# Splitting five exponentials, with their sums and transposes, into two groups in the first unit, and moving a weight sum to GpSimd

## The chip, the cores and the metric

The kernel runs on one core of one Trainium2 chip. The metric is the device time of one execution in microseconds (us), taken as the median of several executions. A profile records one execution; its times count from the start of the span, which is some 2 us shorter than the device time.

Most runs of one kernel lie within 1.6 us of its median, but 11 of the 73 runs come out 5.7 to 7.6 us longer, with the kernel before and with the variants alike (one more, of 939.03, lies between). Two traces that fell on such runs show that the extra time arises in the first 50 us, ahead of everything discussed here (see the last section). I call them late starts.

## The reference, cut to what matters

Eight batches of attention with pooled keys and values, then a two-layer network with a "snake" activation:

```python
k_p, v_p = means of k, v over 8 neighbouring rows        # 576 -> 72 rows
scores = q @ k_p^T / 8; scores -= max(scores)
attn = exp(scores) / sum(exp(scores))
x = (attn @ v_p), heads side by side                      # 4608 x 512
h = x @ w_in                                              # 512 -> 2048
g = h + sin(alpha * h)**2 / alpha
out = g @ w_out                                           # 2048 -> 512
```

Both large products are done by a fast matrix-multiplication scheme (seven products of sub-blocks instead of eight), so sums of blocks of `w_in` are needed before some of the products.

## The kernel before

The first layer runs in nine units of 512 rows. A unit has 28 slots: four groups J of seven products, 8 matmuls each in the trace. Everything else is attached to a slot, and runs in the order in which it is emitted, each engine taking its own work strictly in that order. In the first unit (u = 0) attention for "batch two" (index 1) has to be done beside the products, because the second unit needs its result.

```python
def exp(i):                                   # row block i of five; ScalarE
    nc.scalar.activation(out=e, in_=e, func=AF.Exp, scale=scale)
def norm(i):                                  # sum and reciprocal on VectorE, multiplication (L280) on GpSimd
    nc.vector.tensor_reduce(out=sm[:n], in_=ex[:n, i, :, 0:Sp + 1], axis=AX, op=OP.add)   # L287
    divide(i, sm, nc.gpsimd)
def turn(i):                                  # two 32x32-block transposes on VectorE (L404, L405)
    ...
def move(part):                               # SBUF to SBUF, 8 transfers for each part, all five blocks in each (L416)
    ...
# ... one group G of a unit, the work left over after product k of the slot before:
def left0(): nc.scalar.copy(out=G.b6[:], in_=G.b1[:])                  # L692; then the squares of group Q before
def left1(): self.finish(Q)                                            # L733, two additions on VectorE
def left2(): nc.scalar.copy(b7 <- b6); nc.scalar.copy(p5 <- b5)        # L704, L706
def left3(): sin(G, 0, 0, G.b1); square(G, 0, 0)                       # ScalarE L672, L679
def left4(): add(G.g[:, 1, :, 1], G.b7[:], G.p5[:])                    # L645: must be read before product 4 writes b7
# ... the schedule of the first unit:
at(8, self.combine_w_in, 2, (0, 1, 2, 3), self.nc.gpsimd)              # third part of w_in, four additions (L537)
at(13, self.combine_w_in, 3, (0, 1, 2, 3))                             # fourth part, on VectorE
for i in range(5):
    at((4, 5, 6, 7, 8)[i], A.q_t, i)
    at((7, 8, 9, 11, 12)[i], A.score, i)
    at((14, 14, 15, 15, 15)[i], A.exp, i)
    at((14, 15, 15, 16, 16)[i], A.norm, i)
    at((15, 16, 16, 17, 17)[i], A.turn, i)
# ...
at(17, A.move, 0); at(17, A.move, 1)
at(20, A0.norm_rest); at(23, A0.a_rest)                                # remainder of batch one (L359 to L368, L394)
at(25, lambda: A.values((0, 2, 1, 3), A.free_banks()))                 # products with the values (L456, L458)
```

`Sin` and `Exp` lie in different activation tables. A switch shows in the trace as ACT_TABLE_LOAD; `Square` and copies run between exponentials without one.

## Time and profile before

| | before |
|---|---|
| median | 937.49 us (936.88 to 937.92, 3 runs) |
| profiled span | 935.2 us, clock 0.995 |
| TensorE busy | 914.5 us, 98% |
| waits of TensorE between 64 and 81 us | 1.20 + 0.35 + 5.12 us |
| matmuls at half clock after them | 6.50 us for what takes 3.46 elsewhere |

A "wait" is idle time of an engine just before an instruction; behind the arrow stands what ended it by the profile. With TensorE busy nearly throughout, only its waits (and its clock) can be won. The prediction shows the lines.

### The profile page before, as it was taken

To read this page: it belongs to the slowest core of one execution; us is meant where nothing else is said; L and a number is where in the kernel's file an instruction comes from. 1 tells how busy PE (TensorE), PEld (TensorE's weight loads), DVE (VectorE), ACT (ScalarE), POOL (GpSimd) and SP (SyncE) were. 2 spreads that over 40 slices of the span, in tenths; PEclk is the share of its full clock that TensorE was granted. 3 is DMA by queue.
4 is the path that set the end of the run, shared out by engine and by line. 5 is a ranking of instruction groups with operands and counts; after the bars stand their busy time and mean duration, and the time that the engine had idled before them with its cause. 6 is when DMAs were issued, how large, how long until landed. Compare 5 with 4: busy or idle time off the path is not lost.

```text
span 935.2 us, 17656 instructions
## 1 busy us (share of the span) xinstructions
PE 914.5 (98%) x6953; PEld 817.3 (87%) x6953; DVE 690.6 (74%) x1064; ACT 436.9 (47%) x1009; POOL 152.6 (16%) x150
## 2 busy tenths in 40 slices
PE   7997999999999999999999999999999999999997
PEld 6675787887878788787888899999999999999997
DVE  7578675766757677573456889988888898889794
ACT  3664576675866758677796641111121111111111
POOL 4254160341704316040000000000000000000000
PEclk9998999999999999999999999999999999999999
DMA  9964656756657565545626346252535354443501
GB/s 252 237 200 129 177 167 174 211 158 192 187 170 222 152 181 138 165 145 154 241 75 200 133 141 190 65 173 82 166 89 157 98 144 111 128 126 101 153 14 39
DMA packets 141299, 141.12 MB, mean 151 GB/s; under 512 B 49808, under 2 KB 111008, under 8 KB 141216
## 3 DMA queue, kind: packets, MB, share of 16 engines
q1 hardware_dynamic: 140144, 138.81, 51.3%
q10 hardware_dynamic: 1072, 1.19, 0.4%
q8 instruction: 55, 0.90, 0.4%
q14 instruction: 28, 0.23, 0.1%
HBM read 75.37 MB, written 47.19 MB: 131 GB/s over the span
## 4 chain that ended last, share of the span: by engine, by line
PE 93%; DVE 1%; ACT 1%; POOL 0%; issue 0%; DMA 0%; SPq 0%; DVEq 0%; ACTq 0%; POOLq 0%
PE PS L666 46%; PE PS L963 41%; PE PS L258 3%; PE PS L456 1%; PE PS L458 1%; PE PS L481 0%; ACT s L672 0%; PE PS L478 0%; POOL ex L280 0%; DVE h L733 0%; PE PS L228 0%; DVE sm L287 0%; PE PS L239 0%; DMA out_dram<-o 0%; DVE o L981 0%
## 5 line engine op out<-in xcount | busy, mean ns | idle before, releaser
L666 PE MATMUL PS<-home,a 128*128 128x256 f32 x1152 | 270.4, 386 | 5.5 <-DVE h L645 5.1
L666 PEld LDWEIGHTS PS<-home,a 128*128 128x128 f32 x1152 | 217.2, 192 | 44.1 <-DVE h L645 7.2
L666 PE MATMUL PS<-home,as 128*128 128x256 f32 x864 | 201.1, 382 | 1.2 <-ACT PS L692 1.2
L666 PEld LDWEIGHTS PS<-home,as 128*128 128x128 f32 x864 | 161.6, 190 | 25.3 <-issue 1.6
L963 PE MATMUL PS<-s,wb 128*128 128x144 f32 x896 | 119.3, 286 | 0.4 <-ACT PS L1076 0.4
L963 PEld LDWEIGHTS PS<-s,wb 128*128 128x128 f32 x896 | 113.7, 190 | 0.7 <-ACT PS L1076 0.6
L679 ACT ACTIVATE s<-s,c 128x256 f32<-128x256 f32 (+1 forms) x216 | 110.0, 572 | 0.0
L117 POOL TENSOR_TENSOR kvin<-kvin 96x768 f32<-96x768 f32 (+3 forms) x42 | 69.1, 1644 | 204.8 <-DMA kvin<-in_v_dram 191.3
L645 DVE TENSOR_TENSOR h<-PS,p 128x512 f32<-128x512 f32 x72 | 49.2, 684 | 66.4 <-PE PS L666 33.3
L672 ACT ACTIVATE s<-h,al 128x256 f32<-128x256 f32 x144 | 65.1, 502 | 56.5 <-DVE h L645 56.5
L1076 ACT COPY PS<-PS 128x144 f32<-128x144 f32 x56 | 14.7, 263 | 145.7 <-PE PS L963 144.3
L672 ACT ACTIVATE s<-PS,al 128x256 f32<-128x256 f32 x144 | 60.1, 468 | 40.1 <-DVE h L733 20.0
L963 PE MATMUL PS<-s,a 128*128 128x144 f32 x512 | 73.2, 286 | 0.0
L963 PE MATMUL PS<-r,wb 128*128 128x144 f32 x512 | 73.2, 286 | 0.0
L963 PEld LDWEIGHTS PS<-r,wb 128*128 128x128 f32 x512 | 67.1, 190 | 0.1
L963 PEld LDWEIGHTS PS<-s,a 128*128 128x128 f32 x512 | 67.0, 190 | 0.0
L733 DVE TENSOR_TENSOR h<-PS,s 128x512 f32<-128x512 f32 x36 | 24.6, 683 | 53.3 <-ACT s L679 53.2
L1095 ACT COPY PS<-PS 128x144 f32<-128x144 f32 x56 | 14.7, 263 | 88.5 <-PE PS L963 88.5
L963 PE MATMUL PS<-s,we 128*128 128x144 f32 x384 | 54.9, 286 | 0.0
L963 PE MATMUL PS<-x,wb 128*128 128x144 f32 x384 | 54.9, 286 | 0.0
L963 PEld LDWEIGHTS PS<-s,we 128*128 128x128 f32 x384 | 50.3, 190 | 0.1
L733 DVE TENSOR_TENSOR h<-h,s 128x1024 f32<-128x1024 f32 x36 | 50.3, 1398 | 0.0
(170 smaller groups left out, 1202.3 us busy)
## 6 DMA issues: line engine op xcount, KB each, us to landing
g_bridge<-h SPq DMA_DIRECT2D x72, 512.0 KB
r<-g_bridge SPq DMA_DIRECT2D x31, 1152.0 KB
out_dram<-o SPq DMA_DIRECT2D x128, 72.0 KB
kvin<-in_k_dram SPq DMA_DIRECT2D x14, 576.0 KB
q<-in_q_dram SPq DMA_DIRECT2D x7, 1024.0 KB
kvin<-in_v_dram SPq DMA_DIRECT2D x14, 512.0 KB
aM<-tr SPq DMA_DIRECT2D x56, 100.0 KB
aM<-tr SPq DMA_DIRECT2D x56, 80.0 KB
```

The costliest lines, as they stand in the source:

```text
L117: self.nc.gpsimd.tensor_tensor(out=t[..., 0:w] if w > D else out, in0=t[..., 0:w], in1=t[..., w:2 * w], op=OP.add)
L258: nc.tensor.matmul(ps[e][r:r + q.shape[-1], hp, :], q[s], k, start=True, stop=True)
L456: nc.tensor.matmul(o[64 * e:64 * e + 64], w, x, start=True, stop=False, skip_group_check=True)
L458: nc.tensor.matmul(o, w.rearrange("p e d -> p (e d)"), x, start=False, stop=True, skip_group_check=True)
L645: add = lambda o, x, y: nc.vector.tensor_tensor(out=o, in0=x, in1=y, op=OP.add)
L666: nc.tensor.matmul(ps[:, jj, :], self.A[p][:, kk, f * P:(f + 1) * P], x[:, kk, :], start=(start and jj == 0 and kk == 0), stop=(kk == 1), ...
L672: nc.scalar.activation(out=G.s[:, i, jj, j, :], in_=src[:, jj], func=AF.Sin, scale=self.al[:, f:f + 1])
L679: nc.scalar.activation(out=x, in_=x, func=AF.Square, scale=self.c[:, f:f + 1])
L733: add = lambda o, x, y: self.nc.vector.tensor_tensor(out=o, in0=x, in1=y, op=OP.add)
L963: nc.tensor.matmul(out, W[:, J // 2, J % 2, :], A[:, J, :], start=(start and J == 0), stop=(J == self.NJ - 1), skip_group_check=True)
L1076: nc.scalar.copy(out=x1[:, 0, :], in_=x0[:, 1, :])
L1095: nc.scalar.copy(out=x1[:, 1, :], in_=x1[:, 0, :])
```

## The change

The intent was to break up the burst of softmax work around slots 14 to 17. Two of the five row blocks go through exponential, sum, multiplication and transpose in slots 9 to 13, at the price of one more switch to the exponential's table and back. The fourth part of `w_in` is summed on GpSimd, so that VectorE is free for the transposes. The additions of the third part, on GpSimd already, go behind the first two multiplications (slot 10 instead of 8).

```diff
-            at(8, self.combine_w_in, 2, (0, 1, 2, 3), self.nc.gpsimd)
-            at(13, self.combine_w_in, 3, (0, 1, 2, 3))
             for i in range(5):
                 at((4, 5, 6, 7, 8)[i], A.q_t, i)
                 at((7, 8, 9, 11, 12)[i], A.score, i)
-                at((14, 14, 15, 15, 15)[i], A.exp, i)
-                at((14, 15, 15, 16, 16)[i], A.norm, i)
-                at((15, 16, 16, 17, 17)[i], A.turn, i)
+                at((9, 9, 14, 14, 15)[i], A.exp, i)
+                at((10, 10, 15, 15, 16)[i], A.norm, i)
+                at((13, 13, 16, 17, 17)[i], A.turn, i)
+            at(10, self.combine_w_in, 2, (0, 1, 2, 3), self.nc.gpsimd)
+            at(10, self.combine_w_in, 3, (0, 1, 2, 3), self.nc.gpsimd)
```

## The prediction

> **What bounds the kernel now.** I read the page first: the busy shares and the strip of 40 slices (23.4 us each).
>
> ```profile
> PE 914.5 (98%) x6953; PEld 817.3 (87%) x6953; DVE 690.6 (74%) x1064; ACT 436.9 (47%) x1009; POOL 152.6 (16%) x150
> ...
> PE   7997999999999999999999999999999999999997
> PEclk9998999999999999999999999999999999999999
> ```
>
> TensorE is the bound nearly everywhere. A change that leaves its work alone can only win where it waits. Apart from the two ends, that is the fourth slice (70 to 94 us), which is also the only one with a clock of 8 tenths. It lies in the first unit, the unit that is changed. So the second view is TensorE's timeline there (start, duration, then in brackets the idle time before it and what ended it):
>
> ```profile
> 64.20 1.89 PE L666 MATMUL PS<-home,as 128*128 128x256 f32 x8
> 67.29 1.97 PE L666 MATMUL PS<-home,as 128*128 128x256 f32 x8 [1.20 <-ACT PS L692]
> 69.09 1.89 PE L666 MATMUL PS<-home,a 128*128 128x256 f32 x8
> 71.33 1.97 PE L666 MATMUL PS<-home,a 128*128 128x256 f32 x8 [0.35 <-ACT PS L704]
> 73.13 1.89 PE L666 MATMUL PS<-home,as 128*128 128x256 f32 x8
> 80.14 6.67 PE L666 MATMUL PS<-home,a 128*128 128x256 f32 x16 [5.12 <-DVE h L645]
> 86.64 1.89 PE L666 MATMUL PS<-home,as 128*128 128x256 f32 x8
> ```
>
> Eight matmuls are one slot of the schedule; counting along the rows, 64.20 is slot 15 and 80.14 begins slot 20. Three waits: 1.20 + 0.35 + 5.12 = 6.67 us. A fourth loss is hidden in a duration: the 16 matmuls from 80.14 reach the next row after 6.50 us, where 16 such matmuls elsewhere take 3.46 (60.74 to 64.20). That is 3.04 us more. The view by windows shows why; the numbers after the window's length are busy times of PE, PEld, DVE, ACT, POOL, then the granted clock:
>
> ```profile
> 78.00:80.00 2.00, 0.00 (x0) 0.00 (x0) 1.81 (x5) 0.00 (x0) 2.00 (x2) 0.83 0.00 0
> ...
> 82.00:84.00 2.00, 2.00 (x6) 1.63 (x5) 1.97 (x2) 0.04 (x1) 1.92 (x3) 0.50 0.69 160
> ```
>
> The clock had gone to half during the wait. All there is to win here is 6.67 + 3.04 = 9.7 us, 1.0% of 937.5.
>
> What made the long wait is in the chain of waits (start, duration, engine and line):
>
> ```profile
> 66.12 0.77 DVE sm L287
> ...
> 67.26 1.16 POOL ex L280
> ...
> 71.09 2.63 DVE h L733 x2
> ...
> 77.44 1.15 POOL ex L280
> ...
> 79.51 0.59 DVE h L645
> ```
>
> Slot 20 writes into a bank which the VectorE addition L645 must have read first. VectorE takes its work in order, and ahead of that addition stand the whole of the softmax's end for batch two: five sums with reciprocals, five transposes, each of which waits for GpSimd's multiplication L280, and the additions L733. All of it starts only after the exponentials at 65.40.
>
> **What the Trainium skill says.** "TensorE: Matmul & The Clock Gate", section "What's actually happening": the array falls to half clock after an idle window of about 3.4 us and needs about 3.4 us of work to recover; the window runs freely. The trace agrees: full clock for some 4.3 us of the gap (0.83 over 78 to 80 means half clock from about 79.3), then 0.50 until about 86.1; the wait of 1.20 us cost no clock. "ScalarE: Activation LUTs", section "What ACT_TABLE_LOAD costs": about 1283 ns for the load plus 1380 ns to drain. The trace has 1.28 us, and 1.30 from the load's start to the exponential's (64.11 to 65.40); the drain is not seen as extra time here, so I use 1.28. "GPSIMD Engine Reference", section "4.1 Engine selection": two-input elementwise work is about twice as slow there as on VectorE. The trace: 1.27 us against 0.68 for the same 128x512 addition (L537). "SBUF — State Buffer", section "SBUF: two separate sides": a VectorE instruction with two SBUF inputs and a GpSimd one lock each other out for a whole instruction. The trace fits: the second L733 takes 1.21 us at 108.85, with GpSimd idle, and 2.14 at 71.56 beside L280.
>
> **The change, part by part.**
>
> *First exponentials and their table switch (new, slots 9 to 11).* ScalarE ends its work at 51.37 and then sits idle until this copy, which TensorE releases:
>
> ```profile
> 54.12 0.57 ACT L704 COPY PS<-PS 128x512 f32<-128x512 f32 x1 [2.75 <-PE PS L666]
> ```
>
> One load (1.28) and two exponentials (1.26) are 2.54 us, ending near 53.95: they fit in the 2.75. Going back to sine costs a second load. In the built program the wait for TensorE's slot 10 sits on that load, so it runs from about 55.75 to 57.05 and the sine comes 1.2 us later than its 55.84. ScalarE then waited 1.70 us for VectorE before the next sine at 59.17, so this is absorbed. Nothing reaches TensorE.
>
> *First two sums (now slot 10).* Two times (0.76 + 0.20) less overlap, about 1.75 us on VectorE from 54.95, into an idle stretch of 1.58 us before 56.53. Delay: 0.2 us, passed on down to the copy L692, so the 1.20 wait of slot 16 becomes about 1.35. The second switch to the exponentials stays in that path.
>
> *First two multiplications and both sums of w_in on GpSimd.* GpSimd is free at 56.0. Two L280 of 1.15 end at 58.3; the four additions of part three (1.27 each) end at 63.4. TensorE wants the first results in slot 15 (64.20), ready at 59.6: no wait. The four of part four end at 68.5; they are wanted only from slot 22 on.
>
> *Off VectorE.* Four L537 (2.6 us, at 62.15) disappear; in their place come two transposes of 0.92 us each (0.71 + 0.27 less overlap), which no longer wait.
>
> *What remains after 66 us.* Squares end near 68.6 as before. VectorE: two sums 66.3 to 68.1; L733 68.6 to 70.8 (0.6 + 1.2 + some 0.4 of lock; GpSimd multiplies rows two and three then, ending at 70.7 to 72.0); third transpose to 71.75; fifth sum to 72.7; GpSimd's last multiplication 72.75 to 73.95 beside the fourth transpose; fifth transpose to 75.0, or 75.4 with a full lock; L645 to 75.6 to 76.1. Before, it ended at 80.10.
>
> *TensorE.* Slot 16 at 67.45, then 1.80 per slot; the copy L704 is ready by 70.2, so the 0.35 goes. Slot 19 ends at 74.75. Slot 20 at 75.95, a wait of 1.2 instead of 5.12. That is far from 3.4 us: the clock should stay full and the 3.04 us go too.
>
> *What then comes closer.* Two things were hidden under the slow stretch. First, the remainder of batch one (L359 to L368, 3.65 us of it locked against GpSimd's pooling) is needed at slot 23. TensorE comes there at 81.2, the remainder ends about 81.6: a wait of 0.4. Second, the moves of the transposed rows:
>
> ```profile
> 79.54 10.29 SPq L416 DMA_DIRECT2D aM<-tr  x16
> ```
>
> They start when the fifth transpose ends (79.51) and the DMA strip falls quiet at about 91.1, which is 11.6 us later. From 75.2 that is 86.8. TensorE arrives at the value products (93.54 before): 82.1 + 1.8 + 0.8 + 1.9 = 86.6. A wait of about 0.3. They take 2.95 us, so slot 25's own product starts at 89.9, against 96.49 before: 6.6 us earlier by this sum. After that the work is TensorE's own as before, with the same small waits.
>
> In losses: before 9.7; after 1.35 + 1.2 + 0.4 + 0.3 = 3.25. The two ways give 6.5. I take off 0.3 for small waits that I can't see, and say 6.2.
>
> **Rivals.**
>
> *GpSimd becomes the bound of the chain.* It now has ten instructions in a row from 56.0 to 68.5 before the third multiplication, and the third transpose waits for that. For it: 1.27 us is a figure taken beside VectorE work with a PSUM input, which does not lock. Against it: VectorE has hardly any two-input SBUF work between 56 and 68.5. Two microseconds of delay would be hidden behind L733; if it came 4 us late, the wait would grow to some 3 us, the clock might drop, and the time would be about 935.
>
> *The moves take over.* For it: they need 11.6 us however early TensorE arrives; in the second unit a VectorE transpose (L194) waited 4.69 us for them. If they landed 2 us later than I think, the gain would be some 4.5 us: about 933.
>
> *The early table switch delays TensorE.* Two loads more, 2.6 us. For it: the first group ends 0.15 us before the copy L704 is due. Against: the product that needs the copy starts at 56.34. I expect nothing; at worst 1 us.
>
> *All waits close.* If the moves land early and VectorE is quicker than I have it, only the 1.35 is left: about 929.
>
> **Range and chances.** From 929.3 (nearly everything gone but the slot 16 wait) to 935.0 (the GpSimd rival, or a clock drop that stays). All that can be won is 1.0%, so over 2% faster is all but excluded; 2% slower would take 19 us of new waits in a unit of some 75 us, for which I see no source.
>
> **What would show it.** Right: in TensorE's timeline a wait of 1 to 1.5 us before slot 16, one of 0.5 to 2 us before slot 20 still released by L645, the 16 matmuls after it in about 3.5 us, clock 1.00 throughout; the eight L537 on GpSimd ending at 68 to 69; L416 issued from about 75; short waits for the remainder and the moves. Wrong: a wait of 3 us or more anywhere there with the clock at 0.50 after it, a wait for GpSimd's L537 in slots 15 to 19, or a gain that is lost again before 100 us.

## The result

The changed kernel took 930.98 us (930.28 to 931.20, 4 runs) against 937.18 for the kernel before in the same measurement (935.58 to 937.92, 4 runs): 6.2 us less. The ratio is 0.9935, with a 95% interval from 0.9918 to 0.9952. Ratios are computed as the mean time of one kernel's fast runs over that of the other's of the same rounds, so they are not quite the ratio of the medians. The interval lies clear of 1.

The page of the changed kernel, same rows as before:

```profile
PE 912.3 (98%) x6953; PEld 815.0 (88%) x6953; DVE 687.6 (74%) x1060; ACT 439.8 (47%) x1011; POOL 158.9 (17%) x154
...
PEclk9999999999999999999999999999999999999999
```

TensorE's busy time fell by 2.2 us with the same number of matmuls, and the 8 in the fourth slice of the clock is gone. That part of the gain is not a wait: it is matmuls that no longer run at half speed. (They had lost 3.04 us; a new wait of 1.1 us, shown below, counts as busy.) TensorE's timeline in the stretch (start, duration, idle time before in brackets):

```profile
64.35 1.89 PE L666 MATMUL PS<-home,as 128*128 128x256 f32 x8
67.45 1.96 PE L666 MATMUL PS<-home,as 128*128 128x256 f32 x8 [1.21 <-POOL a L537]
69.25 3.62 PE L666 MATMUL PS<-home,a 128*128 128x256 f32 x16
72.71 1.89 PE L666 MATMUL PS<-home,as 128*128 128x256 f32 x8
75.32 3.72 PE L666 MATMUL PS<-home,a 128*128 128x256 f32 x16 [0.72 <-DVE h L645]
78.87 1.89 PE L666 MATMUL PS<-home,as 128*128 128x256 f32 x8
...
85.87 3.05 PE L456 MATMUL PS<-aM,vm 64*64 64x512 f32 x16
```

The wait of 5.12 us is 0.72, the 16 matmuls behind it reach the next row after 3.55 us (78.87), and the 0.35 us before slot 18 is gone. The wait of 1.21 us before slot 16 has not moved. The last line hides a new wait: 16 value matmuls take 3.05 us where the kernel before has 1.95 (at 93.54). The chain of waits splits them:

```profile
68.60 2.19 DVE h L733 x2
...
74.68 0.59 DVE h L645
...
85.94 1.01 PE PS L456 x4
86.94 0.04 issue
86.98 1.93 PE PS L456 x12
```

Four of these matmuls run, then the twelve others follow at 86.98; so about 1.1 us went by inside that line. These matmuls read the moved rows, and VectorE, which waited for the same moves to let go of their source, resumed at 86.92. Slot 25's own product began at 89.92 instead of 96.49: 6.57 us earlier. The span is 6.1 us shorter; the other 0.4 us was lost later on, nearly all of it at one matmul (at 296.87 us) that comes 0.35 us late. TensorE's waits after 94 us show it; the kernel before has no such line after 100 us:

```profile
PE PS L666 <- DVE h L645: 0.2, 1, 0.2
```

It goes with the move of w_in's fourth part to GpSimd (see e2).

### The profile page after: what moved, and what is told of

The parts are those of the page before. It is cut to its first block, busy times and chain, and to the rows that moved or that the text cites. A ratio compares the mean times of both kernels' runs of the same rounds, so it can differ in the third digit from the quotient of the medians.

```text
span 929.1 us, 17658 instructions
## 1 busy us (share of the span) xinstructions
PE 912.3 (98%) x6953; PEld 815.0 (88%) x6953; DVE 687.6 (74%) x1060; ACT 439.8 (47%) x1011; POOL 158.9 (17%) x154
## 4 chain that ended last, share of the span: by engine, by line
PE 93%; ACT 2%; DVE 1%; issue 0%; DMA 0%; POOL 0%; SPq 0%; DVEq 0%; ACTq 0%; POOLq 0%
PE PS L666 45%; PE PS L963 41%; PE PS L258 3%; PE PS L456 2%; PE PS L458 1%; PE PS L481 0%; ACT s L672 0%; PE PS L478 0%; ACT ex L275 0%; PE PS L228 0%; DVE h L733 0%; DVE h L645 0%; ACT s L679 0%; PE PS L239 0%; DMA out_dram<-o 0%
## 5 line engine op out<-in xcount | busy, mean ns | idle before, releaser
L666 PE MATMUL PS<-home,a 128*128 128x256 f32 x1152 | 267.2, 382 | 1.0 <-DVE h L645 1.0
L666 PEld LDWEIGHTS PS<-home,a 128*128 128x128 f32 x1152 | 215.0, 190 | 38.7 <-issue 5.3
L645 DVE TENSOR_TENSOR h<-PS,p 128x512 f32<-128x512 f32 x72 | 49.2, 684 | 64.2 <-PE PS L666 33.3
L733 DVE TENSOR_TENSOR h<-PS,s 128x512 f32<-128x512 f32 x36 | 24.7, 685 | 50.8 <-ACT s L679 50.7
L963 PEld LDWEIGHTS PS<-x,wb 128*128 128x128 f32 x384 | 50.3, 190 | 0.0
```

The costliest lines, as they stand in the source:

```text
L645: add = lambda o, x, y: nc.vector.tensor_tensor(out=o, in0=x, in1=y, op=OP.add)
L666: nc.tensor.matmul(ps[:, jj, :], self.A[p][:, kk, f * P:(f + 1) * P], x[:, kk, :], start=(start and jj == 0 and kk == 0), stop=(kk == 1), ...
L733: add = lambda o, x, y: self.nc.vector.tensor_tensor(out=o, in0=x, in1=y, op=OP.add)
L963: nc.tensor.matmul(out, W[:, J // 2, J % 2, :], A[:, J, :], start=(start and J == 0), stop=(J == self.NJ - 1), skip_group_check=True)
```

## The experiments

Eight kernels ran, in two sets of four (e1 to e4 and e5 to e8), each set on a chip of its own; all were correct. The kernel before took 936.76 us in the first set (11 runs) and 937.15 in the second (11 runs).

### e1: only the fourth part of w_in goes to GpSimd

```diff
-            at(13, self.combine_w_in, 3, (0, 1, 2, 3))
+            at(13, self.combine_w_in, 3, (0, 1, 2, 3), self.nc.gpsimd)
```

> The kernel before, with only the four additions of the fourth part of w_in moved from VectorE to GpSimd (slot 13); exponentials, sums and transposes stay. My theory: VectorE has nothing to do between these additions and the first sum anyway (it sat idle 1.36 us before 66.12 and waited for the exponential), so freeing 2.6 us of it moves nothing. Expected: 937.2 us, within 0.7 us of before; the wait before slot 20 stays near 5 us, the clock still drops to 0.50. Rival (VectorE's load was the trouble): about 2.6 us of that wait go, and the clock drop with it: 932 to 934.5.

Measured: 937.31 us (936.47, 937.24, 937.38 and a late start of 943.46), ratio 1.0013 (0.9979 to 1.0047). The profiled run was the late start, so its times stand about 6.4 us later, but the pattern is that of the kernel before: 5.13 us of wait before slot 20, and 6.32 us for the 16 matmuls behind it. VectorE shows why nothing was won:

```profile
72.56 0.76 DVE L287 TENSOR_REDUCE sm<-ex 128x8 f32<-128x584 f32 x1 [3.89 <-ACT ex L275]
```

In the kernel before it was idle for 1.36 us in front of this sum. The 2.5 us of additions taken away became 2.5 us more waiting for the exponential. The rival falls.

### e2: the change without the move of w_in's fourth part

```diff
-            at(10, self.combine_w_in, 3, (0, 1, 2, 3), self.nc.gpsimd)
+            at(13, self.combine_w_in, 3, (0, 1, 2, 3))
```

> The changed kernel, but with the fourth part of w_in still summed on VectorE (slot 13). My theory: the gain is all in the exponentials, sums and transposes done early; VectorE's idle 2.29 us before the third sum takes up the 2.5 us of additions. Expected: 931.0 us, within 0.6 us of the changed kernel; wait before slot 20 of 0.5 to 1.2 us, clock 1.00. Rival (both halves of the change are needed): VectorE's chain is 2.5 us later, wait before slot 20 about 3 us: 933 to 935.

Measured: 930.14 us (929.88 to 930.82, 5 runs), ratio 0.9924 (0.9901 to 0.9947). The clock stays full, and the wait before slot 20 is 0.81 us:

```profile
75.04 3.72 PE L666 MATMUL PS<-home,a 128*128 128x256 f32 x16 [0.81 <-DVE h L645]
```

With e1 this settles the second half of the change: moving the fourth part to GpSimd gains nothing, alone or with the rest. By the times alone, whether it costs a few tenths can't be said: this kernel is 6.6 us below the kernel before of its set, and the changed kernel, in another set, is 5.95 below its own (937.15 less 931.20, e8). The traces settle it. From slot 25's own product to the end of the span, the three with the fourth part on VectorE take 838.71 us (before), 838.80 (e2) and 838.74 (e3). The seven with it on GpSimd take 839.12 to 839.26 (changed kernel, e1, e4 to e8). So the move costs 0.4 us. Of that, 0.35 to 0.38 us lies at one matmul that waits for a VectorE addition L645: at 136.95 us in e1, near 297 us in the other six. Why the move should delay an addition so much later is open.

### e3: only the exponentials are split

```diff
-                at((14, 14, 15, 15, 15)[i], A.exp, i)
+                at((9, 9, 14, 14, 15)[i], A.exp, i)
```

> The kernel before, with only the exponentials in two groups (slots 9, 14 and 15); the sums with multiplications and the transposes stay in their old slots, and so does w_in. My theory: what counts is that two sums and two transposes leave the queue ahead of L645; exponentials alone only let the first sum start at 64.7 instead of 66.1. Expected: L645 about 1 to 1.5 us earlier than in the kernel before, a wait before slot 20 of 3.5 to 4.2 us, clock perhaps still dropping: 933.5 to 936. Rival (splitting the burst of exponentials on ScalarE is the gain itself): as the changed kernel, 931.

Measured: 934.65 and 935.34 us, and two late starts of 940.72 and 942.60; ratio with all four 1.0010 (0.9972 to 1.0047), which is therefore inconclusive. The two ordinary runs are some 1.8 us below the kernel before, but two are few. The wait before slot 20 is 4.26 us, just above what I expected. The trace, again of a late start, carries the verdict, if times are counted from slot 16 on. TensorE before slot 20:

```profile
85.27 5.21 PE L666 MATMUL PS<-home,a 128*128 128x256 f32 x16 [4.26 <-DVE h L645]
```

Slot 16 begins at 73.86 here, so slot 20 follows 11.41 us later; in the kernel before that is 12.85 (67.29 to 80.14), in the changed kernel 7.87 (67.45 to 75.32). Of the 4.98 us between the last two, the early exponentials alone bring 1.44. The rest needs the sums (with their multiplications) and transposes to leave VectorE's queue early as well: e2 adds just these, and the later slot of w_in's third part, and has 7.95 (67.09 to 75.04). Sums and transposes were not tried apart. The clock still fell to half here.

### e4: one more switch of tables

```diff
+            at(13, lambda: self.nc.scalar.activation(out=self.dummy[:], in_=self.ident[:, 1:2], func=AF.Exp))
```

(`dummy` is a tile of 128x1, allocated at the start.)

> The changed kernel with one more switch to the exponential's table and back in slot 13, for a dummy exponential of 128x1 whose result nobody reads. It falls into ScalarE's 1.60 us of idle time before the sine at 61.83. My theory: a load costs 1.28 us and nothing else, and the load back waits with the sine for VectorE until about 61.8, so the chain to slot 16 and to L645 comes 1.2 to 1.3 us later: 932.2 us, the wait before slot 16 growing from 1.21 to about 2.4 us. Rival (each switch also costs a drain of 1.38 us, as the Trainium skill's page has it): two switches are 5.3 us, 3.7 us more than the idle time: about 934.7. Second rival (the idle time hides it): 931.0.

Measured: 932.29 to 932.61 us in four runs, and two late starts (938.93 and 939.01); with these, ratio 0.9975 (0.9941 to 1.0009). Four runs at 932.4 against 931.2 for the changed kernel (e8) are 1.2 us more. But e8 ran in the other set; with each taken against the kernel before of its own set, it is 1.6 (4.35 us below it against 5.95). So the cost is near the 1.2 us expected, but it did not come about in the way expected. ScalarE's timeline:

```profile
60.40 1.28 ACT L845 ACT_TABLE_LOAD   x1
61.69 0.20 ACT L845 ACTIVATE dummy<-ident 128x1 f32<-128x1 f32 x1
61.91 1.28 ACT L672 ACT_TABLE_LOAD   x1
63.21 0.91 ACT L672 ACTIVATE s<-h,al 128x256 f32<-128x256 f32 x2
```

Two switches and a tiny exponential take 2.81 us from 60.40 to the next sine; a drain of 1.38 us for each does not show. That rival falls, and so does the one that the idle time hides the switch. But TensorE:

```profile
68.83 3.19 PE L666 MATMUL PS<-home,as 128*128 128x256 f32 x8 [2.88 <-POOL as L537]
```

The wait before slot 16 grew to 2.88 us rather than 2.4 (some 0.45 us of it because VectorE's addition L733 at 51.63 ran into GpSimd's pooling and took 2.00 us instead of 1.51), and the clock fell (it stands before the last two numbers of a row):

```profile
68.00:70.00 2.00, 1.17 (x4) 1.06 (x5) 1.47 (x5) 2.00 (x5) 2.00 (x3) 0.85 0.62 150
70.00:72.00 2.00, 2.00 (x6) 1.53 (x6) 2.00 (x2) 1.10 (x2) 1.06 (x1) 0.50 0.00 0
72.00:74.00 2.00, 2.00 (x9) 1.68 (x8) 1.97 (x6) 1.07 (x2) 0.03 (x1) 0.79 0.47 170
```

Slots 16 to 18 took 6.94 us (68.83 to 75.77) instead of 5.26 (67.45 to 72.71), 1.7 us more. In return the waits before slot 20 (0.72) and for the moves (3.05 us for the value matmuls became 2.19) shrank, because TensorE came later to them. That the sum comes out near the number expected is luck: the errors offset each other.

### e5: the fourth part of w_in later on GpSimd

```diff
-            at(10, self.combine_w_in, 3, (0, 1, 2, 3), self.nc.gpsimd)
+            at(16, self.combine_w_in, 3, (0, 1, 2, 3), self.nc.gpsimd)
```

> The changed kernel with the fourth part of w_in still on GpSimd, but after the last multiplication L280 and before the pooling of the keys, instead of before the third multiplication. The profile of the changed kernel names GpSimd's L537 as what ended the wait of 1.21 us before slot 16; the kernel before named ScalarE's copy L692. My theory: it is still the copy (it ends 0.14 us before the matmul in both traces) and GpSimd's load is harmless. Expected: the wait before slot 16 stays at 1.2 us and is put down to L692; third and fourth multiplication done by about 69.5 instead of 71.8; total 930.7 us, at most 0.5 us better than the changed kernel. Rival (GpSimd's additions hold TensorE): the wait goes and the total is about 929.8.

Measured: 931.29 us (930.28 to 932.47, 6 runs), ratio 0.9918 (0.9885 to 0.9951); no difference from the changed kernel.

```profile
67.89 1.97 PE L666 MATMUL PS<-home,as 128*128 128x256 f32 x8 [1.22 <-ACT PS L692]
```

GpSimd had done its last addition by 63.8 us here, and the wait is as long as ever. So in the changed kernel it is the copy L692, too. The name L537 there only says that an addition happened to end (67.37) a little after the copy (67.31). The small extra that I expected did not come: the second L733 addition was still delayed (1.55 us), because the multiplications, now free to start at 67.86, met it all the same.

### e6: the fifth transpose behind the addition L645

```diff
-                at((13, 13, 16, 17, 17)[i], A.turn, i)
+                at((13, 13, 16, 17, 19)[i], A.turn, i)
@@
-            at(17, A.new_a)
-            at(17, A.move, 0)
-            at(17, A.move, 1)
+            at(19, A.new_a)
+            at(19, A.move, 0)
+            at(19, A.move, 1)
```

> The changed kernel with the fifth transpose and the moves emitted in slot 19, so that the addition L645 that slot 20 waits for stands ahead of the fifth transpose on VectorE (it fits into the 0.55 us in which VectorE waits for GpSimd). My theory: two things end together here, the wait before slot 20 and the landing of the moves, which come 12.3 us after the fifth transpose. The wait of 0.72 us goes, the fifth transpose ends at the same time as before, and TensorE waits that much longer inside the value products (1.1 us becomes about 1.8). Expected total: 930.9, within 0.4 us of the changed kernel. Rival (the wait before slot 20 is worth its length): 930.2.

Measured: 931.33 us (930.74 to 931.88, 6 runs), ratio 0.9918 (0.9885 to 0.9951). TensorE has no wait before slot 20 any more (its slots 19 and 20 follow each other). At the value products:

```profile
86.31 1.07 PE L456 MATMUL PS<-aM,vm 64*64 64x512 f32 x4 [0.27 <-DMA aM<-tr]
87.58 1.93 PE L456 MATMUL PS<-aM,vm 64*64 64x512 f32 x12 [0.19 <-DMA aM<-tr]
```

Now the profile names the moves itself. The time is that of the changed kernel (931.20 in e8's five ordinary runs). A wait of 0.72 us was removed, and most of it came back. From the start of slot 24 to L458, 5.40 us pass here (84.04 to 89.44) and 4.91 in the changed kernel (83.94 to 88.85), which is 0.5 us more for the moves. Another 0.2 us came back at the small transposes of batch one's remainder (0.73 us from 80.62 to 81.35, instead of 0.56). Between slots 15 and 25 this trace is still 0.3 us shorter than that of the changed kernel (25.25 against 25.57); the times do not show it.

### e7: a version meant to beat both

```diff
-                at((9, 9, 14, 14, 15)[i], A.exp, i)
-                at((10, 10, 15, 15, 16)[i], A.norm, i)
-                at((13, 13, 16, 17, 17)[i], A.turn, i)
+                at((9, 9, 10, 15, 15)[i], A.exp, i)
+                at((10, 10, 13, 16, 16)[i], A.norm, i)
+                at((13, 13, 17, 17, 17)[i], A.turn, i)
...
-            at(10, self.combine_w_in, 3, (0, 1, 2, 3), self.nc.gpsimd)
+            at(16, self.combine_w_in, 3, (0, 1, 2, 3), self.nc.gpsimd)
```

> A version meant to beat both: the third exponential joins the first group (slot 10, behind the copies L704 and L706, without a further switch), the fourth and fifth go behind the copy L692 (slot 15), sums in slots 10, 10, 13, 16, 16, transposes in 13, 13, 17, 17, 17, and the fourth part of w_in after the last multiplication. My theory: the wait before slot 16 (1.21 us) goes, because no table load stands ahead of L692; only two of five rows are left in the chain to L645, which ends near 73.3 instead of 75.25; the fifth transpose ends near 72.5 instead of 74.7 and the moves land 2.2 us earlier. Expected total: 928.8, range 928.2 to 930.0. Rival (the copy L704 now stands behind three exponentials and a load, and delays slot 18): the 1.2 us turn up there, and the gain over the changed kernel is under 1 us: 930.2.

Measured: 928.55 to 929.92 us in five runs (median 929.28), and one late start of 935.92; with all six the ratio is 0.9909 (0.9871 to 0.9947). The changed kernel beside it (e8) has 930.63 to 931.92 in its five ordinary runs: the ranges do not meet, and the difference is 1.9 us. It beats both kernels.

```profile
70.85 1.97 PE L666 MATMUL PS<-home,a 128*128 128x256 f32 x8 [0.45 <-ACT PS L704]
...
80.78 0.27 PE L395 MATMUL PS<-ident,last 64*128 64x64 f32 x1 [0.60 <-DVE last L368]
...
85.59 1.95 PE L456 MATMUL PS<-aM,vm 64*64 64x512 f32 x16
```

The wait before slot 16 is gone, because the copy L692 now stands ahead of the table load. The rival was right in part: 0.45 us came back before slot 18, since L704 stands behind that load instead. The moves no longer hold the value matmuls (1.95 us, as in the kernel before). And the remainder of batch one, L368, now holds TensorE for 0.60 us. These two are the half microsecond by which it missed 928.8, and more.

### e8: the changed kernel once more

> The changed kernel itself, on the same chip and in the same rounds as the three other runs of this set, to compare them with: 931.0 us, within 0.5 us.

Measured: 930.63 to 931.92 us in five runs (median 931.20), and one late start of 937.07; with all six the ratio is 0.9928 (0.9888 to 0.9969). In this trace the wait before slot 16 is 1.46 us and is put down to L692.

## Why the prediction was right

The time on record was 931.3 us, and 930.98 was measured. The steps, in the prediction's order:

- **What there is to win.** Three waits and the half clock, 9.7 us together. Confirmed: 6.57 us of it were gone by slot 25, and the clock was full.
- **The early table switch is hidden.** ScalarE's load, two exponentials and the way back:

```profile
51.55 1.28 ACT L275 ACT_TABLE_LOAD   x1
...
54.27 0.57 ACT L704 COPY PS<-PS 128x512 f32<-128x512 f32 x1 [0.17 <-PE PS L666]
...
55.98 1.28 ACT L672 ACT_TABLE_LOAD   x1 [0.63 <-issue]
```

  0.17 us of the 2.75 us gap were left, where I had 0.15. TensorE was not touched. (All times of this trace stand 0.16 us later than before from 17 us on; that is not the change.)
- **The wait before slot 16.** I said 1.35 us; it is 1.21, as before. The 0.2 us of delay by the early sums did not come through to the copy.
- **GpSimd.** Ten instructions in a row from 56.26 to 68.6; I had said 56.0 to 68.5.
- **The chain to L645.** L733 ended at 70.79 (70.8 predicted), and the fifth transpose at 74.68 (75.0 to 75.4). L645 ended at 75.27, where I had 75.6 to 76.1, so the wait before slot 20 was 0.72 us and not 1.2. The lock between VectorE and GpSimd that the Trainium skill's "SBUF — State Buffer", section "SBUF: two separate sides", describes held, and cost about what I had put in (0.4 us): the second L733 took 1.22 us with GpSimd idle (82.33), 1.58 beside L280 (69.21) and 2.15 in e1.
- **The clock.** Full throughout, as expected. The longest wait is now 1.21 us; e4 shows that 2.88 was already too long.
- **The remainder of batch one.** I had a wait of 0.4 us; there was none worth counting. TensorE came at 80.69, and only the last of its five small transposes needs L368, which ended at 80.99.
- **The moves.** This is the one mis-sized term: 0.3 us predicted, about 1.1 us measured. That the moves would land near 86.8 was right (86.94). They take 12.3 us from the end of the fifth transpose (74.68), of which issuing alone is 10.6:

```profile
74.71 10.62 SPq L416 DMA_DIRECT2D aM<-tr  x16
```

  I had read 11.6 us off the trace before. Of the 0.7 us between 11.6 and 12.3, 0.3 is slower issue (10.62 against 10.29); the rest lies between the last issue and the release of the matmuls, 1.6 us here, where I had stopped at the end of the traffic. And TensorE arrived at 85.87, 0.7 us sooner than I had it. What the other waits fell short of my estimates was therefore paid here. That is why the sum was right (89.9 for slot 25, 89.92 measured) although three of its terms were too large and one too small: the moves set the time at slot 25. e6 shows this for most of such a wait.
- **Luck.** That the moves landed where I had them is luck in part: the fifth transpose came 0.5 us early, and they took 0.7 us longer. So is the fit of the last step: the 0.3 us that I took off for small waits unseen met the 0.4 us that moving w_in's sum cost later, which I had not foreseen.

The rivals that I had set against it were that GpSimd becomes the bound of the chain (no: e5 relieves it for the third and fourth multiplication and nothing changes), that the moves take over (yes, in part), that the early switch delays TensorE (no), and that all waits close (no; e7 comes nearer).

Which part of the change brought it: the exponentials together with their sums and transposes (e2 has all of the gain). The exponentials alone bring 1.4 us of the 5.0 us at slot 20 (e3). The sum of w_in on GpSimd brings nothing (e1, e2) and by the traces costs 0.4 us later on.

## What to carry to other kernels

When an engine takes its work in order, look at what stands in its queue ahead of the one instruction that the bottleneck waits for; here moving two of five row blocks into an earlier idle stretch was worth some 6 us, and taking 2.5 us of other work off the same engine was worth nothing. A wait of a few microseconds before matmuls can cost more than half as much again in clock (3.04 us after a wait of 5.12, 1.7 after 2.88), so it is worth closing even if a shorter one remains. Before counting a removed wait as gain, follow what else is due soon after: here transfers that take 12 us from their start took over most of a wait of 0.7 us (e6).

## What the Trainium skill lacked or had wrong

- "ScalarE: Activation LUTs", section "What ACT_TABLE_LOAD costs": the page adds a drain of about 1380 ns to each load of about 1283 ns. Here a load costs 1.28 us and the next activation starts within 0.03 us of its end; two loads and a dummy exponential of 0.20 us took 2.81 us in all (e4).
- "TensorE: Matmul & The Clock Gate", section "What's actually happening": an idle window of about 3.4 us is given for the fall of the clock. In e4 an idle time of 2.88 us was enough. By the mean clock of 0.85 over 68 to 70 us, the fall came near 69.4, about 0.6 us after work had been resumed (68.83), and by 0.79 over 72 to 74 it lasted until about 72.8. The page's 3.4 us of recovery fit. For the fall, a wait shorter than the window was not safe here. The list of granted clocks in the packed traces (no view of `prof` prints it) shows why the same wait need not always do it: each change lies a whole number of steps of 3.413 us after the first entry (e4: 7.98, then 69.42 and 72.83; before: 7.63, then 79.31 and 86.13). The step that ended at the fall in e4 began near 66.0; it held 2.8 us of idle time and 0.6 us of matmuls, and so was not wholly idle.
- The same page and section, on the warm-up at the start: about 3.4 us of sustained work are given. In the late starts of e1 and e3 TensorE was busy for 3.5 of each 4 us from 8 us on, and yet its matmuls took 1.7 times as long up to about 20 us. The same line in e3 and in the kernel before:

```profile
12.40 1.24 PE L329 MATMUL PS<-h,q 64*64 64x72 f32 x32 [0.62 <-ACT h L298]
```

```profile
10.54 0.73 PE L329 MATMUL PS<-h,q 64*64 64x72 f32 x32 [0.73 <-ACT h L298]
```

  In e3 the first unit starts at 28.57 us instead of 24.96; a wait of 2.73 us for the pooled keys follows (L229). The profile's clock column says 1.00 there, but it has nothing to go by: the list of granted clocks in the packed trace begins at 20.05 us in e3 and 20.20 in e1, at 7.63 in the kernel before, and in all three the matmuls take their full-speed times from about then on. That the other runs with some 6 us more are of the same kind is inferred from their times alone; why the clock stays low is open.
- No page has a measured time, on this chip, for issuing one such transfer from SyncE's queue; what the pages say of set-up is rough. Here 16 moves of 80 to 100 KB take 10.3 to 10.8 us to issue, about 0.65 us each. Bandwidth does not set when they land: over 76 to 86 us of the changed kernel the DMA engines are busy 56 to 65% of the time and move 123 to 154 GB/s, and over the next 2 us, with larger transfers, 95% and 321 GB/s.
